# An mLSTM cell and a gated feed-forward in one kernel: another order of the first slot's rounding, sigmoid and transfers

## The chip, the cores and the metric

The kernel runs on one core of a Trainium2 chip. The metric is the device time of one execution in microseconds (us). The profiled core's TensorE clock was granted at 0.981 of full speed on average.

## The reference, cut to what matters

An mLSTM recurrence over 768 steps for 4 batches and 8 heads of 40 dimensions, then a feed-forward whose activation is h·cos(h):

```python
for t in range(S):
    m_new = np.maximum(f_gate[:, :, t] + m, i_gate[:, :, t])
    f_stab = np.exp(f_gate[:, :, t] + m - m_new)
    i_stab = np.exp(i_gate[:, :, t] - m_new)
    C = f_stab * C + i_stab * outer(vt, kt)
    n = f_stab * n + i_stab * kt
    y[:, :, t] = sigmoid(o_gate) * (C @ qt) / maximum(abs(n . qt), 1)
x = y.transpose(0, 2, 1, 3).reshape(B * S, H * D)      # 3072 x 320
h = x @ w_in                                           # 320 x 2048
out = (h * cos(h)) @ w_out                             # 2048 x 320
```

## The kernel before, in words

**Cells.** The sequence is cut into 6 chunks c of 128 steps. A chunk of one batch b is a cell n = 4c + b; there are 24. A cell computes scores (q times k, TensorE), weighs them with decays E (weigh, VectorE), multiplies by the values (values, TensorE), updates a state (seam, state) and normalises (normalize or normalize_turned). The result goes to xT, the input of the feed-forward for chunk c.

**Feed-forward.** Chunk c's feed-forward runs in 8 steps f2, each 2 times 128 of the 2048 columns. A step is an `Up`: matmuls of w_in with xT into two PSUM banks (L636, L639); then for each bank a rounding on ScalarE (near, L644), a subtraction on VectorE (rest, L647), a sine on ScalarE (sin, L652) and a product on VectorE (gate, L656). Both banks are free again after the gates, and only then may the next Up write them. The down step before it (down, L668) multiplies the gates by w_out.

**Slots.** After the head (first_cells: cells 0 to 3, in a hand-written order), both_parts(c, b) runs two Ups (i = 0 and i = 1) beside cell n = 4(c + 1) + b. The first slot is both_parts(0, 0), with cell 4 and the first two Ups of chunk 0; it also prepares cell 5. Each engine takes its instructions in the order in which the code names them; nothing is reordered. So an instruction that waits holds all that stands behind it on its engine.

**Weights.** w_in and w_out arrive as 64-bit floats and are made into float32 here. weights_in(f) loads the bits of 512 columns in three pieces (8 transfers of 128 KB and 4 of 64 KB, L139 and L174), weights_out(p) those of two row blocks in one (640 KB, L180). take_apart runs on ScalarE (L150, L152), put_together on VectorE (L157 to L161) and, last, on GpSimd (L162); to_float32 is both. `pieces` and `outs` hold what is loaded and not yet converted; next_out converts the next piece of w_out and loads another.

**Transfers.** All loads are issued by SyncE, in order, into one hardware queue; each is given one of eight completion slots in turn and waits for the transfer that had the slot before. load_E(n) brings the running maxima for a cell's decays (512 KB, L354), and for an even cell also the factors G for two cells (two times 256 KB, L360). load_two(n) brings q and k of two cells ("qk", L339) or k and v of two cells ("Kv", L344). The buffers ks2 and vs2 hold two cells each. load_o(1) brings the o gates of chunk 1 in 8 transfers (L309), and sigmoid(1) (L318, L320) turns them for all four cells of that chunk; turn_gate (L460) transposes them for one cell.

**For the next cell.** decay_exponents (L391, GpSimd) masks E, decay (L405, ScalarE) takes eight exponentials, weigh_k (L410) scales k, odd_values (L416, GpSimd) copies the upper dimensions of the values for an even cell and the odd one behind it, turn_blocks (L455, VectorE) transposes q and k of one cell, scale_q (L464, GpSimd) makes qG from the transposed q and G; values(n) reads qG and the copied values. clear_low (L440) zeroes two buffers once. sin_next (L938) makes ScalarE load the sine's table ahead of time. ScalarE loads a table whenever exponential, sigmoid and sine follow each other.

```python
def odd_values(n):
    if n % 2 == 0:
        src = vs2[n // 2 % 2].rearrange("q n (a g) d -> q (n a) g d", g=2)[:, :, :, 32:D]
        nc.gpsimd.tensor_copy(out=vr2[n // 2 % 2].rearrange("q n a g d o -> q (n a) g d o")[:, :, 0:3:2, :, 0], in_=src)
```

warm(k) issues k matmuls with zeros, which write a bank that nobody reads.

Of the kernel before, what the change touches and what calls it, by code (L numbers as in the profile page):

```python
# [29 lines left out]
def kernel(  # L30
# [23 lines left out]
    C = 128  # L54
# [87 lines left out]
    def to_float32(dst, bits):  # L142
        take_apart(dst, bits)
        put_together(dst, bits)
# [178 lines left out]
    def load(n, which="qkv"):  # L323
        c, b = divmod(n, B)
        for name, dst, src in (("q", qs(n), q), ("k", ks(n), k), ("v", vs(n), v)):
            if name in which:
                nc.sync.dma_start(out=dst[:, :, 0:D], in_=src[b, :, ts(c, C)].rearrange("h t d -> t h d"))

    def load_two(n, which="qkKv"):
        c, b = divmod(n, B)  # L330
        m = n // 2 % 2
        for name, src in (("q", q), ("k", k)):
            if name in which:
                src = src.rearrange("b (p j) (c t a) d -> j c t (b p) (a d)", j=2, a=C // 32, t=32)
                for j in range(2):
                    for low in range(1 if n < 2 * B else 2):
                        x = 0 if low else 32
                        dst = raws[name][m][64 * j + 32 * low:64 * j + 32 * low + 32, x:x + WR]
                        nc.sync.dma_start(out=dst.rearrange("t (p x) -> t p x", x=C // 32 * D),  # L339
                                          in_=src[j, c, :, 4 * b:4 * b + 8])  # L340
        for name, dst, src in (("K", ks2[m], k), ("v", vs2[m], v)):
            if name in which:
                src = src.rearrange("b h (c t) d -> c t b h d", t=C)
                nc.sync.dma_start(out=dst[:, :, :, 0:D], in_=src[c, :, b:b + 2])  # L344
# [472 lines left out]
    def first_cells():  # L817
        nc.vector.memset(nil, 0.0)
        gates_in()
        nc.scalar.copy(out=ident_b, in_=ident)  # L820
        load(0, "qk")
        later_gates_in()
        load(0, "v")
        load(1, "qk")
        load_o(0, (0, 1))
        load(1, "v")
        load(2, "qk")
        load_E(0)
        load_E(1)
        warm(12)  # L830
        wall_in(0, 0, pmu)
        wall_in(0, 1, psum_o())
        gates_first()
        gates_first_out()
        spread(0, 0)
        decay_exponents_half(0, 0)
        turn(0)
        turn_out(0, False)
        gates_sums()
        spread(0, 1)  # L840
        decay_exponents_half(0, 1)
        decay(0)
        weigh_k(0)
        load_E(2)
        load(2, "v")
        load_E(3)
        load_o(0, (2, 3))
        load(3)
        pieces.extend(weights_in(0))
        wall_in(1, 0, psum_o())  # L850
        wall_in(1, 1, psum_o())
        gates_less_sums()
        spread(1, 0)
        decay_exponents_half(1, 0)
        scores(0)
        gates_maxima()
        turn(1)
        weigh(0)
        sigmoid(0, slice(0, 2))
        turn_out(1, False)  # L860
        spread(1, 1)
        decay_exponents_half(1, 1)
        gates_exponents()
        decay(1)
        weigh_k(1)
        values(0)
        normalize(0)
        scores(1)
        gates_exp()
        turn(2)  # L870
        turn_out(2, False)
        warm(2)
        seam(0)
        weigh(1)
        seam_out(0)
        state(0)
        load_two(B, "qk")
        decay_exponents(2)
        gates_diagonal()
        decay(2)  # L880
        weigh_k(2)
        values(1)
        load_E(B)
        normalize(1)
        scores(2)
        turn(3)
        sigmoid(0, slice(2, 4))
        seam(1)
        load_two(B, "Kv")
        load_E(B + 1)  # L890
        load_o(1)
        outs.append((0, weights_out(0)))
        weigh(2)
        decay_exponents(3)
        turn_out(3)
        seam_out(1)
        values(2)
        decay(3)
        weigh_k(3)
        state(1)  # L900
        normalize(2)
        scores(3)
        pg = gates_turn()
        warm(1)
        seam(2)
        weigh(3)
        to_float32(*pieces.pop(0))
        decay_exponents(B)
        pieces.extend(weights_in(1))
        outs.extend((p, weights_out(p)) for p in range(1, 3))  # L910
        seam_out(2)
        state(2)
        for piece in pieces[0:2]:
            take_apart(*piece)
        gates_keep(*pg)
        values(3)
        normalize(3)
        put_together(*pieces.pop(0))
        warm(3)
        seam(3)  # L920
        seam_out(3)
        put_together(*pieces.pop(0))
        low_dimensions(B)
        turn_blocks(B)
        state(3)
        load_E(B + 2)
        decay(B)
        sigmoid(1)
        weigh_k(B)
        odd_values(B)  # L930
        scale_q(B)
# [14 lines left out]
    def both_parts(c, b):  # L946

        n = (c + 1) * B + b
        cell = n < N
        for i in range(2):  # L950
            f2 = 2 * b + i
            up = Up(c, f2)
            if cell and i == 0:
                scores(n)
                if c == 0 and b == 0:

                    warm(8, psum_o())
            if cell and i == 1:
                if n % 2 == 1 and n > B + 1 and n + 3 < N:
                    load_two(n + 3, "Kv")  # L960
            for e in range(2):
                up.near(e)
            for e in range(2):
                up.rest(e)
            if i == 0:
                if cell:
                    weigh(n)
                    if n + 1 < N:
                        decay_exponents(n + 1)
                    if n == B:  # L970
                        clear_low()
                for e in range(2):
                    up.sin(e)
                    up.gate(e)
                if c > 0:
                    sums(c, f2)
                if b == 0 and 0 < c < NC - 1:
                    sigmoid(c + 1)

                if c == 0 and b > 0 and pieces:  # L980
                    to_float32(*pieces.pop(0))
                if c == 0:
                    next_out()
                if cell and n + 1 < N:
                    decay(n + 1)
            else:
                if cell:
                    seam_out(n)
                if pieces:
                    to_float32(*pieces.pop(0))  # L990
                if cell:
                    state(n)
                for e in range(2):
                    up.sin(e)
                    up.gate(e)
                if c > 0:
                    sums(c, f2)
                if n == B + 1:
                    low_dimensions(n + 1)
                while pieces:  # L1000
                    to_float32(*pieces.pop(0))
                if cell and n + 1 < N:
                    weigh_k(n + 1)
                    odd_values(n + 1)
            down_slot(c, f2)
            if (c, f2) == (1, 0):
                weight_sums(1)
            if cell and i == 0:
                turn_gate(n)
                values(n)  # L1010
                seam(n)
                normalize_turned(n)
                fade(n)
                if n % 2 == 1 and n > B + 1 and n + 3 < N:
                    load_two(n + 3, "qk")
                if n > B + 1 and n + 3 < N:
                    load_E(n + 3)
                if b == B - 2 and c + 2 < NC:
                    load_o(c + 2)
                if c == 0 and pieces:  # L1020
                    to_float32(*pieces.pop(0))
                sin_next()
            if f2 == 0 and c > 1:
                for p in range(2):
                    combine(c - 1, p)
            if i == 1:
                if c == 0 and b + 2 < B:
                    pieces.extend(weights_in(b + 2))
                    load_two((n + 3) // 2 * 2)
                    load_E(n + 3)  # L1030
                if cell and n + 1 < N:
                    turn_blocks(n + 1)
                    scale_q(n + 1)
                if c == 0:
                    next_out()
                if (c, f2) == (0, LAST):
                    weight_sums(0)
# [41 lines left out]
```

## Time and profile before

| | |
|---|---|
| time, median of 3 runs | 556.17 us (553.79 to 556.29) |
| profiled execution: span from the first to the last instruction | 549.6 us |
| what lies around the span (runs less the span) | 4.1 to 6.6 us |
| PE / DVE / ACT / POOL busy | 522.2 / 420.0 / 280.4 / 235.3 us |
| first slot, first Up | 41.6 to 47.7 us |
| first slot, second Up | 58.2 to 63.0 us |
| DMA over the span | 57.81 MB, 105 GB/s |

The profiled execution has no time of its own beside its span; the three runs were timed without a profile. PE is TensorE, DVE VectorE, ACT ScalarE, POOL GpSimd, SP SyncE. A line of the timeline gives start, length, engine, source line, operation, the tiles written and read, the shape, how many, and in brackets how long the engine had been idle before and what ended that. A row of the windows gives the stretch, its length, each engine's busy time with the number of instructions, the granted clock of PE (1.00 is full), the mean busy share of the 16 DMA engines and GB/s. A share over 1 means that packets overlapped on an engine.

### The profile page before, as it was taken

The numbers are of one execution on the slowest core, as the hardware profiler recorded it, in microseconds if no ns is written. First come the engines' busy times: TensorE is split into PE (matmuls) and PEld (weight loads), VectorE is DVE, ScalarE is ACT, GpSimd is POOL, SyncE is SP. The second block draws the span as 40 slices with busy tenths as digits, with TensorE's granted clock in tenths as the row PEclk, the third lists the DMA queues.
The fourth block names the chain that finished last, engine by engine and source line by source line (L and its number), as shares of the span: only waits on it lengthen the run. The fifth ranks groups of instructions, "written<-read, shape, count | busy, mean of one in ns | idle before, by whom it ended". The sixth has DMA issues, their size and how long they took to land.

```text
span 549.6 us, 10494 instructions
## 1 busy us (share of the span) xinstructions
PE 522.2 (95%) x3844; PEld 348.6 (63%) x3844; DVE 420.0 (76%) x906; ACT 280.4 (51%) x537; POOL 235.3 (43%) x381
## 2 busy tenths in 40 slices
PE   7997989989979999999999999999999999999996
PEld 4873554546646666756766756766756757575755
DVE  5864999997877787887886888787887878674645
ACT  2867966847455445555535555535556533231311
POOL 7535456463784545534444435444423421221211
PEclk9968899999999999999999999999999999999999
DMA  9998878687926538318438428338410000010001
GB/s 135 228 201 224 244 163 215 137 188 186 163 92 155 72 92 187 41 67 202 49 93 183 44 67 199 52 92 181 47 69 25 5 6 6 1 48 1 1 1 48
DMA packets 99939, 57.81 MB, mean 105 GB/s; under 512 B 62304, under 2 KB 92608, under 8 KB 99888
## 3 DMA queue, kind: packets, MB, share of 16 engines
q1 hardware_dynamic: 96496, 55.64, 47.2%
q10 hardware_dynamic: 3248, 1.33, 1.1%
q8 instruction: 30, 0.49, 0.4%
q14 instruction: 21, 0.17, 0.1%
q0 software_dynamic: 144, 0.18, 0.1%
HBM read 51.71 MB, written 4.11 MB: 102 GB/s over the span
## 4 chain that ended last, share of the span: by engine, by line
PE 65%; DVE 11%; ACT 9%; POOL 5%; DMA 3%; issue 3%; SPq 3%; ACTq 0%; DVEq 0%; POOLq 0%
PE pup L636 24%; PE acc L746 21%; PE pup L639 7%; PE late L746 2%; PE ps L482 2%; DVE n L647 2%; ACT E L405 2%; DVE g L656 2%; PE vt L517 2%; PE po L668 2%; PE vt L508 1%; ACT n L644 1%; DMA E<-M_d 1%; DVE st L619 1%; DVE t L455 1%
## 5 line engine op out<-in xcount | busy, mean ns | idle before, releaser
L636 PE MATMUL pup<-xT,w_in_sb 128*128 128x512 f32 x384 | 178.8, 609 | 8.2 <-DVE g L656 7.8
L644 ACT ACTIVATE n<-pup 128x512 int32<-128x512 f32 x96 | 52.2, 595 | 206.4 <-PE pup L639 206.3
L647 DVE SCALAR_TENSOR_TENSOR n<-pup,n 128x512 f32<-128x512 f32 x96 | 61.8, 686 | 91.2 <-ACT n L644 91.2
L636 PEld LDWEIGHTS pup<-xT,w_in_sb 128*128 128x128 f32 x384 | 70.6, 192 | 84.2 <-issue 61.2
L710 POOL TENSOR_TENSOR D<-g 128x128 f32<-128x128 f32 x40 | 19.8, 495 | 178.6 <-DVE g L656 156.7
L652 ACT ACTIVATE n<-n 128x512 f32<-128x512 f32 x96 | 58.5, 631 | 18.5 <-DVE n L647 14.7
L656 DVE SCALAR_TENSOR_TENSOR g<-pup,n 128x512 f32<-128x512 f32 x96 | 61.7, 685 | 2.1 <-ACT n L652 0.4
L746 PE MATMUL acc<-w_out_sb,g 128*128 128x160 f32 x320 | 59.0, 305 | 0.0
L746 PE MATMUL acc<-T,g 128*128 128x160 f32 x320 | 58.3, 302 | 0.0
L639 PE MATMUL pup<-xT,w_in_l 64*128 64x512 f32 x192 | 54.2, 641 | 0.0
L746 PEld LDWEIGHTS acc<-w_out_sb,g 128*128 128x128 f32 x320 | 47.4, 190 | 6.8 <-issue 4.5
L746 PEld LDWEIGHTS acc<-T,g 128*128 128x128 f32 x320 | 47.8, 190 | 4.4 <-issue 3.8
L405 ACT ACTIVATE E<-E,tab 128x128 f32<-128x128 f32 x160 | 49.2, 391 | 2.0 <-POOL E L391 1.7
L668 PE MATMUL po<-w_out_sb,g 128*128 128x320 f32 x128 | 36.6, 439 | 3.8 <-POOL w_out_sb L162 3.7
L639 PEld LDWEIGHTS pup<-xT,w_in_l 64*128 64x128 f32 x192 | 14.4, 184 | 36.5 <-issue 34.3
L746 PE MATMUL acc<-T,S 128*128 128x160 f32 x160 | 35.3, 302 | 0.0
L538 POOL TENSOR_TENSOR yt<-yt,db 128x128 f32<-128x128 f32 x20 | 10.9, 545 | 55.0 <-DVE db L533 55.0
L668 PEld LDWEIGHTS po<-w_out_sb,g 128*128 128x128 f32 x128 | 23.7, 190 | 16.4 <-POOL w_out_sb L162 4.5
L482 PEld LDWEIGHTS ps<-t,t 40*128 40x128 f32 x384 | 24.8, 188 | 10.9 <-issue 8.0
L488 DVE TENSOR_TENSOR E<-ps,E 128x512 f32<-128x512 f32 x48 | 30.7, 681 | 0.0
L464 POOL TENSOR_TENSOR qG<-t,G 128x512 f32<-128x512 f32 x20 | 25.7, 1285 | 10.2 <-DVE t L455 10.0
L746 PE MATMUL acc<-w_out_sb,S 128*128 128x160 f32 x160 | 29.1, 301 | 0.0
(176 smaller groups left out, 902.5 us busy)
## 6 DMA issues: line engine op xcount, KB each, us to landing
E<-M_d SPq DMA_DIRECT2D x22, 512.0 KB
qr<-in_q_dram SPq DMA_DIRECT2D x36, 160.0 KB
kr<-in_k_dram SPq DMA_DIRECT2D x36, 160.0 KB
G<-G_d SPq DMA_DIRECT2D x20, 256.0 KB
bits<-in_moe_w_out_dram SPq DMA_DIRECT2D x8, 640.0 KB
bits<-in_moe_w_in_dram SPq DMA_DIRECT2D x32, 128.0 KB
out_dram<-o_sb SPq DMA_DIRECT2D x24, 160.0 KB
ks<-in_k_dram SPq DMA_DIRECT2D x10, 320.0 KB
```

Of the source, the lines that this page charges most:

```text
L405: nc.scalar.activation(out=Es[n][:, h], in_=Es[n][:, h], func=AF.Exp, scale=-1.0, bias=tab[:, c, 0, g:g + 1])
L464: nc.gpsimd.tensor_tensor(out=qG, in0=qkT[n][0], in1=Gs[n], op=OP.mult)
L482: nc.tensor.matmul(ps[j][:, p], kT[r, p], qT[r, p], start=True, stop=True)
L488: nc.vector.tensor_tensor(out=w, in0=pss[n][j], in1=w, op=OP.mult)
L636: nc.tensor.matmul(pu, w_in_sb[:, i, ts(2 * f2 + e, 128)], x(i), start=(i == 0), stop=False)
L639: nc.tensor.matmul(pu, w_in_l[r, f2], x(NK, r), start=False, stop=True)
L644: nc.scalar.activation(out=self.n[e], in_=self.pu[e], func=AF.Copy, bias=0.25)
L647: nc.vector.scalar_tensor_tensor(out=self.n[e].bitcast(FP), in0=self.pu[e], scalar=0.25, in1=self.n[e], op0=OP.add, op1=OP.subtract)
L652: nc.scalar.activation(out=r, in_=r, func=AF.Sin, scale=TWO_PI_DOWN)
L656: nc.vector.scalar_tensor_tensor(out=g, in0=self.pu[e], scalar=TWO_PI, in1=self.n[e].bitcast(FP), op0=OP.mult, op1=OP.mult)
L668: nc.tensor.matmul(po[c][b], gs[c, f][:, ts(b, C)], w_out_sb[:, f], start=(f == 0), stop=(f == NF - 1))
L746: nc.tensor.matmul(a, lhs, rhs, start=start, stop=stop)
```

## The change

In the head: k and v of cells 4 and 5 come in two pairs of transfers (load_one) and no longer in one pair; w_out's first piece is loaded ahead of the o gates; w_in's second group is loaded ahead of E for cell 5, and cell 5's k and v come behind E and w_out's second piece. values(3) and a put_together stand ahead of seam(2). One warm(3) becomes warm(1), so two warm matmuls fall away. sigmoid(1) leaves the head.

In the first slot: sigmoid(1) stands behind the first Up's sines and the conversion of w_out's first piece, where decay(5) stood; decay(5) and one more sin_next stand behind the second Up's gates; turn_blocks(5) moves from the end of the slot to behind the first Up's gates. All other slots keep their order. Lines of the changed kernel are 5 higher from load_two on.

```diff
+    def load_one(n):
+        c, b = divmod(n, B)
+        for dst, src in ((ks(n), k), (vs(n), v)):
+            nc.sync.dma_start(out=dst[:, :, 0:D], in_=src[b, :, ts(c, C)].rearrange("h t d -> t h d"))
...
         seam(1)
-        load_two(B, "Kv")
-        load_E(B + 1)
+        load_one(B)
+        outs.append((0, weights_out(0)))
         load_o(1)
-        outs.append((0, weights_out(0)))
...
         warm(1)
-        seam(2)
         weigh(3)
         to_float32(*pieces.pop(0))
         decay_exponents(B)
         pieces.extend(weights_in(1))
-        outs.extend((p, weights_out(p)) for p in range(1, 3))
-        seam_out(2)
-        state(2)
+        load_E(B + 1)
+        outs.append((1, weights_out(1)))
+        load_one(B + 1)
+        outs.append((2, weights_out(2)))
         for piece in pieces[0:2]:
             take_apart(*piece)
         gates_keep(*pg)
         values(3)
+        put_together(*pieces.pop(0))
+        seam(2)
+        seam_out(2)
+        state(2)
         normalize(3)
-        put_together(*pieces.pop(0))
-        warm(3)
+        warm(1)
         seam(3)
...
         decay(B)
-        sigmoid(1)
         weigh_k(B)
         odd_values(B)
         scale_q(B)
...
                 for e in range(2):
                     up.sin(e)
                     up.gate(e)
+                if (c, b) == (0, 0):
+                    turn_blocks(n + 1)
...
-                if cell and n + 1 < N:
+                if (c, b) == (0, 0):
+                    sigmoid(1)
+                elif cell and n + 1 < N:
                     decay(n + 1)
...
                 while pieces:
                     to_float32(*pieces.pop(0))
+                if (c, b) == (0, 0):
+                    decay(n + 1)
+                    sin_next()
...
                 if cell and n + 1 < N:
-                    turn_blocks(n + 1)
+                    if (c, b) != (0, 0):
+                        turn_blocks(n + 1)
                     scale_q(n + 1)
```

## The prediction

> **What bounds it now.** I read the windows first, then the timeline of the stretch that the diff touches (36 to 84 us), then the landing records of the transfers. The windows' columns are length, busy us of each engine, PE's granted clock, DMA share, GB/s.
>
> ```profile
> 37.00:52.00 15.00, 13.06 (x67) 6.60 (x66) 6.86 (x14) 9.00 (x25) 8.89 (x9) 0.76 1.07 218
> 52.00:60.00 8.00, 5.52 (x76) 4.20 (x77) 7.40 (x14) 7.94 (x15) 1.58 (x1) 0.79 0.67 228
> 60.00:100.00 40.00, 35.78 (x201) 19.82 (x200) 37.44 (x77) 28.18 (x54) 23.66 (x26) 1.00 0.84 199
> 100.00:150.00 50.00, 48.13 (x367) 28.52 (x367) 43.19 (x82) 32.19 (x57) 26.24 (x28) 1.00 0.83 169
> ```
>
> Up to 52 us the DMA queue is full. From 60 us DVE works 37.4 of 40 us, and after 100 us PE 48.1 of 50: what is late at 80 us is late at the end, for nothing later idles long enough to take it up. The first slot stalls here (start, length, engine, line, [idle before it]):
>
> ```profile
> 46.55 1.13 PE L639 MATMUL pup<-xT,w_in_l 64*128 64x512 f32 x4
> ...
> 49.08 1.28 ACT L318 ACT_TABLE_LOAD   x1 [2.60 <-issue]
> 50.37 1.06 ACT L318 ACTIVATE og<-o 128x1024 f32<-128x1024 f32 x1
> ...
> 51.87 1.09 ACT L644 ACTIVATE n<-pup 128x512 int32<-128x512 f32 x2
> ...
> 52.50 1.29 DVE L647 SCALAR_TENSOR_TENSOR n<-pup,n 128x512 f32<-128x512 f32 x2 [7.27 <-ACT n L644]
> ...
> 54.48 0.66 PE L508 MATMUL vt<-E,vs 128*32 128x128 f32 x8 [4.08 <-issue]
> ```
>
> The first Up is ready at 47.7, but its rounding (L644) stands behind the sigmoid, which waits for the o transfers until 48.8. DVE then waits 7.3 us and PE 4.1 before cell 4's values (L508).
>
> **What the change removes.** The rounding moves ahead of the sigmoid. It could start at 47.4 (first Up: PE frees 0.3 us earlier, since two warm matmuls of the head fall away), rest and weigh follow, and values(4) could start at 49.8, right behind the eight warm matmuls, not at 54.5. That alone is 4.7 us on PE.
>
> **What it adds: a wait on POOL.** POOL works in order, and in this stretch it has:
>
> ```profile
> 45.06 0.30 POOL L416 COPY vr<-vs 128x128 f32<-128x128 f32 x1
> 45.31 1.27 POOL L464 TENSOR_TENSOR qG<-t,G 128x512 f32<-128x512 f32 x1
> 46.53 1.09 POOL L391 TENSOR_SCALAR_AFFINE_SELECT E<-E 128x1024 f32<-128x1024 f32 x1
> ```
>
> odd_values(4) (L416) copies the odd values of cells 4 and 5 together, from the buffer vs. Before, one transfer brings both and lands at 42.74. Now cell 5's values are a transfer of their own, issued behind w_in's second group, E of cell 5 and w_out's second piece; it stands ahead of odd_values in the program, and in the changed program's waits the copy waits for it. Behind the copy on POOL stand qG(4), which values(4) need on PE; the select for cell 5, two memsets and w_out's first piece; and DVE's transposes for cell 5, now in the first half of the slot, overwrite what qG(4) reads, so they wait as well, with all of DVE's work behind them.
>
> **When do cell 5's values land (T)?** The trace's last landings of each transfer in the full queue: G 39.48, k and v of cells 4 and 5 42.74, E of cell 5 45.28, o 48.79, w_out 51.55, w_in 56.94, next w_out 59.21. The gaps are the prices: E 2.54, o 3.51, w_out 2.76 and 2.27, w_in 5.39. A single cell's k or v (L327 in the head) lands 0.83 to 1.2 us behind the one ahead of it, so a pair costs about 1.9. In the new order: 39.48 + 1.9 + 2.76 + 3.51 + 5.39 + 2.54 + 2.27 + 1.9 = 59.75. That is the upper end. Before, the queue was not full in part of this:
>
> ```profile
> 52.00:54.00 2.00, 0.00 (x0) 0.00 (x0) 1.50 (x3) 1.98 (x3) 0.00 (x0) 1.00 0.69 178
> 54.00:56.00 2.00, 1.52 (x32) 1.55 (x35) 2.00 (x4) 1.99 (x4) 0.00 (x0) 0.63 0.24 79
> 56.00:58.00 2.00, 2.00 (x42) 1.62 (x36) 1.93 (x5) 1.98 (x3) 0.00 (x0) 0.52 0.71 251
> ```
>
> The missing shares (0.31, 0.76 and 0.29 of 2 us) are 2.7 us; if the new order, with E behind the small pieces, fills all of it, T is 57.0. I take 58.5, a little over the middle: the sum is of measured gaps, the refill is only argued.
>
> **From T to the end.** POOL: copy 0.30, qG 1.28, gaps: qG(4) is done at T + 1.65 = 60.15.
>
> DVE from there, all in a row: transposes for cell 5, 2.05 (69.90 to 71.93 before); w_out's first piece 1.9; oT 0.9; normalize_turned 3.0; w_in's piece 1.9. So the second Up's rest (L647) starts at 69.9; before at 63.75.
>
> PE: 28 of values(4)'s 32 pairs are left, 2.84 at half clock (54.48 to 57.70 was the whole at 3.2) and 0.6 for seam(4): the second Up starts at 63.6. PE was idle from 50.2 to 60.15, which halves the clock. Before, a 4.1 us idle stretch was followed by 3.4 us at half (granted clock 0.63 and 0.52 in the windows above, 1.00 around them), and the full clock came back after 3.4 us of unbroken work. On that 3.4 us raster full clock is back at 64.8, and the second Up (4.75 at full) ends at 68.95; if the part-filled stretch to 61.4 were enough, 1.3 us sooner. Rounding it takes 0.75 until DVE can go on: 69.7. So DVE and PE arrive together, at 69.9, whichever way the clock goes: **6.15 late**. The Trainium skill (TensorE: Matmul & The Clock Gate, Part 1) says that the gate opens after a busy window of some 3.4 us and closes after an idle one, the windows running free. By that rule the part-filled window does not count and the sum is as it stands; by the other reading it would be 0.5 lower, as ACT would run ahead of DVE. The one gap before agrees with the rule (half for 3.41 us); a part-filled window no run here shows.
>
> Up to the second gate nothing else changes order, so gate is at 73.8 (67.70 + 6.1) and the third Up runs 74.4 to 79.2. DVE then lacks the transposes (2.05 saved). But ACT now has cell 5's decay here: it ends the sines at 72.85, w_in_l 0.75, exp's table 1.28, eight exponentials 2.46, the sine's table again 1.28 + 0.1, and only then w_out's second piece, 78.75 to 80.2. (Before, that piece was taken apart at 67.3, and the decay at 56.8 to 60.6.) One table load more in all, 1.28, lies in this row. DVE finishes the piece at 81.4, POOL at 83.0, before 76.30: down's second step is 6.7 late. Third rest 81.4 (74.51), third gate 83.95 (76.91): 6.9 to 7.0 late. From the fourth Up on all orders are as before.
>
> Other edits: values(3) ahead of seam(2) and the earlier w_in pieces on ACT and DVE move the first Up by 0.6 us or less, and E of cell 5 lands near 56; both lie under the wait up to 60.15 and cost nothing; without that cover the first would save 0.3. The o transfers come about 1 us earlier, w_out about 7; both lie under it too. SP issues two transfers more (0.45 each), behind a full queue. ACT's two xT transfers now wait for a landing each of cell 5's values and of E of cell 6 (T + 2.0 + 3.3 = 63.8), which is over before ACT gets there at 70. POOL's four pieces behind the wait (select 1.1, memsets 2.4, w_out 1.6, yt 0.5, fade 2.1) end at 70.4, ahead of w_in's pieces that it needs at 69.9 to 71.7: up to 0.5 of slack used, no more.
>
> **Sum:** T - 51.65 = **+6.85** at T = 58.5: a span of 549.6 + 6.85 = 556.45, and with what lies around it (549.6 against the median's 556.17, 6.6) **563.0**. At T = 57.0 and with the clock early +4.8, at 59.75 +8.1. The no-gain point is T = 51.65.
>
> **Rivals.**
> 1. *The queue drains at its best rate.* The best two microseconds moved 403 GB/s (58 to 60). The 4352 KB from G to cell 5's values (4.46 MB) would then take 11.1 us: T = 50.5, 1.1 faster, 555.0: not slower. It decides from 51.65 down. Against it: 37 to 52 us moved 218 GB/s at a share of 1.07, for most packets are under 512 B (62304 of 99939). The Trainium skill (DMA: Bandwidth & Descriptors, Specifications) gives about 358 GB/s as a core's share of HBM; an estimate from that is T = 51.9 and no change. The trace's full windows lie well under it. Chance 0.09, times from 555 to 559.
> 2. *The wait does not bind* (the copy goes with cell 4's values alone). Then DVE runs through from 47.9, and the second rest comes at 61.65; but the decay on ACT still holds w_out's second piece until 71.4, POOL ends it at 74.2, and down's second step gains 2.1: 554.2. So even the change as meant gives 2 us of the 4.7. Against it: the program's waits. Chance 0.06, half of it under 553.4.
> 3. *Worse:* SP itself is held, as at 33.91, where issuing one v transfer took 4.64 us (another at 78.52 took 2.01); ahead of cell 5's values this would put T 2 to 4.6 later, 565 to 567.6. Chance 0.08. For it: many small rows. Against it: each transfer is half as large now.
>
> **Numbers.** Forecast 0.77, rivals 0.09, 0.06, 0.08. 0.5% is 2.8 us, about what a measurement of this kernel tells from no change. Slower 0.85 (forecast and 3), within it 0.12 (1 and half of 2), faster 0.03. The range, 557.5 to 565.5, takes in both ends of T and of the clock, part of 1 and the near part of 3.
>
> **What would show it.** Right: L416's copy (now L421) with some 12 us of idle POOL before it, released by vs at 57 to 60; PE idle near 10 us inside values(4); the cell 5 transposes on DVE right behind qG(4), at 60; rounding of the first Up at 47 to 48; w_out's second piece on ACT behind a table load, near 79. Wrong: the copy at 45, or cell 5's values landing before 54; or a slot from 84 to 100 us in which the lateness shrinks, which would mean slack that I did not see.

## The result, and the profile after

The changed kernel takes **560.57 us** (median of four runs, 559.63 to 563.25) against 556.07 for the kernel before (four runs beside it, 553.79 to 556.29). The medians differ by 4.5 us. The ratio, taken from all these runs, is 1.0112 with a 95% interval of 1.0076 to 1.0148, which is 6.2 us (4.2 to 8.2): slower, by about 1%. The forecast was 563.0. The profiled execution took 560.36 us with a span of 558.6, which leaves 1.8 us around the span; the spans of the two profiles differ by 9.0 us, twice what the medians differ by. The run before_again below tells why.

The windows of the changed kernel, with the columns as before (length, PE, PEld, DVE, ACT, POOL busy, granted clock, DMA share, GB/s):

```profile
37.00:52.00 15.00, 11.14 (x88) 5.88 (x87) 9.47 (x18) 12.48 (x30) 4.25 (x4) 0.92 0.97 198
52.00:60.00 8.00, 0.00 (x0) 0.00 (x0) 0.00 (x0) 4.17 (x8) 0.00 (x0) 0.56 0.95 211
60.00:100.00 40.00, 33.53 (x232) 19.53 (x233) 34.51 (x70) 24.62 (x48) 23.88 (x26) 0.92 0.77 186
100.00:150.00 50.00, 47.30 (x301) 26.80 (x300) 43.77 (x87) 31.33 (x59) 24.34 (x28) 1.00 0.71 164
```

From 52 to 60 us PE, DVE and POOL do nothing at all; before, PE and DVE worked 5.5 and 7.4 of those 8 us. The queue is full (share 0.95 to 0.97) and moves 198 to 211 GB/s. From 52 to 60 us it is fuller than before (0.95 against 0.67) and yet moves less (211 against 228 GB/s). The timeline of the first slot says what they wait for:

```profile
45.96 1.08 ACT L649 ACTIVATE n<-pup 128x512 int32<-128x512 f32 x2
...
60.37 0.30 POOL L421 COPY vr<-vs 128x128 f32<-128x128 f32 x1 [17.54 <-DMA vs<-in_v_dram]
60.62 1.26 POOL L469 TENSOR_TENSOR qG<-t,G 128x512 f32<-128x512 f32 x1
...
61.92 1.14 DVE L460 STREAM_TRANSPOSE t<-qr 128x512 f32<-128x512 f32 x1 [11.60 <-POOL qG L469]
...
61.94 0.66 PE L522 MATMUL vt<-qG,st 128*32 128x128 f32 x8 [12.93 <-POOL qG L469]
...
81.20 1.14 DVE L157 TENSOR_SCALAR w_out_sb<-w_out_sb 128x640 f32<-128x640 f32 x1 [2.32 <-ACT w_out_sb L150]
...
83.86 1.56 POOL L162 TENSOR_TENSOR w_out_sb<-w_out_sb,bits 128x640 int32<-128x640 int32 x1 [1.87 <-ACT n L649]
```

The rounding (L649) comes 5.9 us sooner than before, right behind the first Up, as the change means it to. Some 1.3 of these 5.9 us are not the change's: the first Up's eight large matmuls took 3.67 us in place of 4.98, for the granted clock was at full from 39.4 us on in this execution and from 44.3 in the one before. Then POOL's copy (L421) waits 17.5 us for the v transfer, and DVE and PE wait 11.6 and 12.9 us for the qG behind it. In the page's table of groups the same idle time stands alone in two lines; its last columns are the idle time before a group and what ended most of it:

```profile
L522 PE MATMUL vt<-qG,st 128*32 128x128 f32 x480 | 24.8, 280 | 12.9 <-POOL qG L469 12.9
L460 DVE STREAM_TRANSPOSE t<-qr 128x512 f32<-128x512 f32 x20 | 22.0, 1101 | 12.5 <-POOL qG L469 11.6
```

480 matmuls of that form in the whole kernel have 12.9 us of idle time before them, and one wait made all of it.

| us from the span's start | before | predicted | after |
|---|---|---|---|
| sigmoid's table in the head (L314) | 25.41 | | 26.24 |
| first Up's rounding | 51.87 | 47.4 | 45.96 |
| cell 5's values have landed (T) | 42.74 | 58.5 | 60.23 |
| qG(4) is done | 46.58 | 60.15 | 61.88 |
| second Up's rest | 63.75 | 69.9 | 72.33 |
| w_out's second piece ends on POOL | 76.29 | 83.0 | 85.42 |
| third rest | 74.51 | 81.4 | 83.64 |
| third gate | 76.91 | 83.95 | 86.03 |
| span | 549.6 | 556.45 | 558.6 |

T is read from the landing records of the trace. From the third gate to the end both profiles take the same (472.7 and 472.6): nothing is made up later. In other executions that stretch takes up to 3.7 us more; before_again shows where.

### The profile page after: what moved, and what is told of

Read it like the earlier page. It is cut to its first block, busy times and chain, and to the rows that moved or that the text cites. A ratio compares the mean times of both kernels' runs of the same rounds, so it can differ in the third digit from the quotient of the medians.

```text
span 558.6 us, 10488 instructions
## 1 busy us (share of the span) xinstructions
PE 520.5 (93%) x3842; PEld 347.3 (62%) x3842; DVE 422.5 (76%) x906; ACT 281.2 (50%) x539; POOL 235.2 (42%) x381
## 2 busy tenths in 40 slices
DMA packets 99971, 57.81 MB, mean 104 GB/s; under 512 B 62336, under 2 KB 92640, under 8 KB 99920
## 4 chain that ended last, share of the span: by engine, by line
PE 60%; DVE 12%; ACT 8%; DMA 6%; POOL 6%; SPq 4%; issue 3%; ACTq 0%; DVEq 0%; POOLq 0%
PE pup L641 23%; PE acc L751 20%; PE pup L644 7%; PE late L751 2%; DMA bits<-in_moe_w_out_dram 2%; DVE n L652 2%; PE ps L487 2%; DMA vs<-in_v_dram 2%; ACT E L410 2%; PE vt L522 2%; DVE g L661 1%; PE vt L513 1%; SPq L139 1%; DVE t L460 1%; DVE st L624 1%
## 5 line engine op out<-in xcount | busy, mean ns | idle before, releaser
L649 ACT ACTIVATE n<-pup 128x512 int32<-128x512 f32 x96 | 52.1, 594 | 219.2 <-PE pup L644 219.1
L657 ACT ACTIVATE n<-n 128x512 f32<-128x512 f32 x96 | 58.5, 629 | 18.3 <-DVE n L652 14.5
L751 PEld LDWEIGHTS acc<-w_out_sb,g 128*128 128x128 f32 x320 | 47.4, 190 | 6.8 <-issue 4.5
L522 PE MATMUL vt<-qG,st 128*32 128x128 f32 x480 | 24.8, 280 | 12.9 <-POOL qG L469 12.9
L460 DVE STREAM_TRANSPOSE t<-qr 128x512 f32<-128x512 f32 x20 | 22.0, 1101 | 12.5 <-POOL qG L469 11.6
```

Of the source, the lines that this page charges most:

```text
L522: nc.tensor.matmul(vt[32 * a:32 * a + 32, i], state[:, ts(HP * i + a, 32)], Gs[n][:, a], start=False, stop=True)
L649: nc.scalar.activation(out=self.n[e], in_=self.pu[e], func=AF.Copy, bias=0.25)
L657: nc.scalar.activation(out=r, in_=r, func=AF.Sin, scale=TWO_PI_DOWN)
L751: nc.tensor.matmul(a, lhs, rhs, start=start, stop=stop)
```

## The experiments

The theory: the copy's wait for cell 5's values is the whole loss. The main rivals: the changed order of the computing makes it (cell 5's decay with one more table load ahead of w_out's second piece, the transposes in the first half), or the clock that falls to half while PE waits. Times of the kernel before differ a little from one measurement to the next, so each run is set against the kernel before in its own.

**before_again** is the kernel before, unchanged.

> The kernel before, unchanged, to learn what its span and its first slot are in another execution. The changed kernel's four runs have spans 1.75 us under their times. If that holds for this kernel too, its profiled execution of 549.6 was a quick one, and its runs at 554 to 556 have spans of 552 to 554.5. The other reading, that a span lies 4 to 6.6 us under the time for this kernel, expects 549.6 again beside a time near 556.

554.02 us; ratio 0.9997 (0.9975 to 1.0018). All its runs, and the 30 of the kernel before beside it, have a span 1.7 to 1.9 us under the time; spans go from 549.1 to 554.6. So the first profile, 549.6, was one of the quickest executions, some 551.4 us long. This run's profile has a span of 554.6, and 4.9 us of the 5.0 are there when the first Up ends. Its windows in the head:

```profile
15.00:20.00 5.00, 5.00 (x23) 4.30 (x21) 2.96 (x4) 3.77 (x6) 3.58 (x6) 0.50 1.05 256
20.00:25.00 5.00, 5.00 (x31) 4.70 (x31) 1.72 (x7) 2.14 (x3) 1.91 (x3) 0.50 0.91 169
25.00:30.00 5.00, 5.00 (x44) 4.00 (x42) 2.36 (x4) 2.66 (x8) 2.13 (x2) 0.67 0.90 214
```

The clock (third figure from the end) is at half for most of this stretch; in the first profile it was 1.00 up to 30 us, and at half from there to 44. The sigmoid's table is loaded at 30.69 (25.41), and the first Up ends at 52.61 (47.68). The o transfers land at the same time in both (48.69 and 48.79), so a late head shortens the wait that the change is aimed at. In before_again:

```profile
55.20 1.29 DVE L647 SCALAR_TENSOR_TENSOR n<-pup,n 128x512 f32<-128x512 f32 x2 [4.70 <-ACT n L644]
```

The rest comes 2.6 us behind the first Up, against 4.8 in the first profile; the second rest is 66.45, only 2.7 later than there. So the kernel makes up nearly half of the late head. At the third gate 2.75 us are left, at the fourth 4.3, and from 172 us on it is 5.0. The fourth gate is later because the down step (L668) behind the third Up ran partly at half clock in this profile (granted clock 0.50 from 79.55 to 82.96 us, first line) and not in the first profile (second line):

```profile
79.10 6.26 PE L668 MATMUL po<-w_out_sb,g 128*128 128x320 f32 x16 [2.19 <-POOL w_out_sb L162]
```

```profile
76.34 4.57 PE L668 MATMUL po<-w_out_sb,g 128*128 128x320 f32 x16 [2.18 <-POOL w_out_sb L162]
```

The wait ahead of it was the same. The changed kernel's profile has 4.57 us there too; the profiles of turn_back, copy_split, v_late and warm_fill have 5.98, 6.26, 6.26 and 7.34. The time from the third gate to the end lies between 472.6 and 476.3 us in the kept profiles; this step makes 1.4 to 2.8 us of the difference where it is slow.

**copy_split** takes the wait away and leaves all else.

```diff
-        if n % 2 == 0:
+        if n in (B, B + 1):
+            src = vs(n).rearrange("q (a g) d -> q a g d", g=2)[:, :, :, 32:D]
+            nc.gpsimd.tensor_copy(out=vr2[n // 2 % 2][:, n % 2, :, 0:3:2, :, 0], in_=src)
+        elif n % 2 == 0:
```

> The changed kernel, but odd_values copies each cell's half by itself: cell 4's where the copy stands now, cell 5's one part later, where the same line is called for cell 5. The result stays the reference's. All transfers and orders stay as changed. Theory 1 (the copy's wait for cell 5's values is the whole loss): cell 4's copy starts near 45 us in place of 60.4, PE does not idle over 2 us inside values(4), the second rest comes at 61.5 to 63 in place of 72.3, the third gate at 75 to 77 in place of 86.0, and the time is 553 to 555.5. Theory 2 (the loss lies in the order: decay(5) behind one more table load, ahead of w_out's second piece, and E of cell 5 late): the third gate stays over 82 and the time over 557.

554.74 us; ratio 1.0014 (0.9987 to 1.0042). The loss is gone with the wait. Cell 4's copy is back at its place, cell 5's comes in the second half of the slot:

```profile
42.62 0.24 POOL L421 COPY vr<-vs 128x64 f32<-128x64 f32 x1
...
72.05 0.25 POOL L421 COPY vr<-vs 128x64 f32<-128x64 f32 x1
```

The second rest is at 62.99, as expected, and the third gate at 77.58, 0.6 us outside what was expected. The span is 552.7, 3.1 over the first profile: 0.7 of it is there at the third gate, and 2.4 more at the fourth, 1.7 of them from the down step at half clock.

**compute_only** and **transfers_only** are the two halves of the change. The first is the changed kernel with these lines as they were, the second the kernel before with these lines alone:

```diff
-        load_two(B, "Kv")
-        load_E(B + 1)
-        load_o(1)
-        outs.append((0, weights_out(0)))
+        load_one(B)
+        outs.append((0, weights_out(0)))
+        load_o(1)
...
         pieces.extend(weights_in(1))
-        outs.extend((p, weights_out(p)) for p in range(1, 3))
+        load_E(B + 1)
+        outs.append((1, weights_out(1)))
+        load_one(B + 1)
+        outs.append((2, weights_out(2)))
```

> The changed kernel with the old transfers: k and v of cells 4 and 5 in one pair, E of cell 5 and w_out where they were. What is left of the change is the order of the computing. Theory 1 (the wait for cell 5's values, which comes from the transfers' order alone): values land near 43, the copy does not wait, the time is 553 to 555.5. Theory 2 (the order of decay(5), sigmoid and transposes costs): 557 to 560.

> The kernel before with the changed order of transfers alone; the computing keeps its old order, so the first Up's rounding still stands behind the sigmoid and cell 5's transposes at the end of the slot. Theory 1: the copy waits for cell 5's values until 58 to 60.5 here too, the third gate comes at 84 to 86.5, the time is 558.5 to 562. Theory 2 (the computing's order makes the loss): the copy's wait lies beside other work, the time is 555 to 557.

compute_only: 553.75 us, ratio 0.9996 (0.9975 to 1.0017). transfers_only: 558.62 us, ratio 1.0076 (1.0045 to 1.0107), with the copy at 60.10 behind 15.0 us of idle POOL and the third gate at 83.63, 0.4 sooner than expected. The order of the computing costs nothing by itself, and brings nothing; the order of the transfers makes the loss.

**v5_w_out** and **v5_w_in** move the landing alone: compute_only with cell 5's v as a transfer of its own, behind w_out's first piece or behind w_in's second group. E of cell 5 and the k transfers stay early.

```diff
-        load_two(B, "Kv")
+        load_two(B, "K")
+        load_v(B)
         load_E(B + 1)
         load_o(1)
         outs.append((0, weights_out(0)))
+        load_v(B + 1)
```

This is v5_w_out; in v5_w_in the last line stands behind `pieces.extend(weights_in(1))`. load_v(n) is load_one(n) without k.

> The changed order of computing with the old transfers (as in the run compute_only, 553.75), but cell 5's v is a transfer of its own behind w_out's first piece; k of both cells and E of cell 5 stay early. Only the landing T of cell 5's values moves. Theory 1 (the wait costs what T lies behind the point where cell 4's values would start, and nothing before that): T is 50.5 to 52, the copy waits until then where the head was quick and not where it was slow, the time is 553.5 to 556. Theory 2 (it is the late E of cell 5 and the pieces behind it that cost, not the copy's wait): as compute_only, 553 to 554.5. The two overlap here; the run v5_w_in parts them.

> As v5_w_out, but cell 5's v behind w_in's second group. Theory 1: T is 56.5 to 58.5, the copy on POOL waits until then whichever way the head ran, the qG matmuls of cell 4's values start some 1.7 us behind T, the time is 556 to 559. Theory 2 (the late E of cell 5, not the copy's wait): E is early here, so 553 to 554.5.

| | T | time | ratio (interval) |
|---|---|---|---|
| compute_only | 42.70 | 553.75 | 0.9996 (0.9975 to 1.0017) |
| v5_w_out | 50.89 | 553.82 | 1.0003 (0.9981 to 1.0025) |
| v5_w_in | 57.81 | 558.99 | 1.0104 (1.0074 to 1.0135) |

Each ratio is against the kernel before in the same measurement. Up to 50.9 us the landing costs nothing, at 57.8 it costs 1.04%, 5.8 us. In v5_w_in PE waits as it does in the changed kernel, with E of cell 5 there since 45.42, so that no late E can be the cause:

```profile
57.86 0.30 POOL L425 COPY vr<-vs 128x128 f32<-128x128 f32 x1 [13.77 <-DMA vs<-in_v_dram]
...
59.43 0.66 PE L526 MATMUL vt<-qG,st 128*32 128x128 f32 x8 [10.22 <-POOL qG L473]
```

The second rest is at 69.83, which is T + 12.0; the changed kernel has T + 12.1.

**v_mid** and **v_late** move cell 5's k and v within the changed kernel.

```diff
+        load_one(B + 1)
         load_E(B + 1)
         outs.append((1, weights_out(1)))
-        load_one(B + 1)
         outs.append((2, weights_out(2)))
```

This is v_mid; in v_late the line stands behind the last one shown.

> The changed kernel with k and v of cell 5 issued ahead of E of cell 5 and of w_out's second piece (right behind w_in's second group), so the 3.5 and 1.9 us that those two took in the queue no longer lie ahead of them. Theory 1 (everything from the copy on moves with the landing T, one for one): T is 54.5 to 55.5 in place of 60.23, the copy starts at once behind it, the third gate comes some 5 us sooner than 86.0, near 81, and the time is 555 to 557. Theory 2 (the loss is not T's): the third gate stays over 84 and the time over 559.

> The changed kernel with k and v of cell 5 issued one transfer later, behind w_out's third piece. Theory 1: T is 61.8 to 62.8, the third gate 1.6 to 2.6 later than 86.0, the time 562 to 563.5. Theory 2 (the loss is not T's): 559.5 to 561.

v_mid: 558.33 us, ratio 1.0088 (1.0059 to 1.0117). T is 55.27 and the copy starts at 55.32, as expected, but the third gate comes at 84.27, not near 81: a miss. E of cell 5, now behind, lands at 58.06, and POOL's select and two memsets follow it. Beside them DVE's first operation on w_out, 0.48 us when alone, takes 2.99:

```profile
58.12 1.09 POOL L396 TENSOR_SCALAR_AFFINE_SELECT E<-E 128x1024 f32<-128x1024 f32 x1 [1.28 <-DMA E<-M_d]
...
58.84 2.99 DVE L157 TENSOR_SCALAR w_out_sb<-w_out_sb 128x640 f32<-128x640 f32 x1
...
59.16 1.19 POOL L445 MEMSET qr<- 128x1312 f32 x1
...
60.29 1.19 POOL L445 MEMSET kr<- 128x1312 f32 x1
```

It ends 0.35 us behind the second memset. The time, 558.33, missed the 555 to 557 as well. This execution also had a late head (first Up ended at 52.41) and its third Up ran at half clock (6.42 us for the eight large matmuls), so it is no clean measure of T's price. v_late: 563.01 us, ratio 1.0181 (1.0147 to 1.0216). The time is as expected, but not for the reason given: T did not move (59.97), since E came earlier in that execution, and the third gate is at 85.77, no later than in the changed kernel. The profile's longer span (561.0) comes from behind it, 1.7 us of it from the down step at half clock. The run says nothing on the price of T.

**warm_fill** keeps PE at work during the wait: 60 warm matmuls in place of 8 ahead of cell 4's values.

```diff
-                    warm(8, psum_o())
+                    warm(60, psum_o())
```

> The changed kernel with 60 warm matmuls in place of 8 ahead of cell 4's values, so that PE works through the wait and its clock does not fall to half; the wait itself stays. Theory 1 (the wait holds DVE and POOL, and DVE sets the second rest; PE's half clock from 53 to 66.7 us lies beside it): the second Up ends 1 to 2 us sooner, the second rest stays within 0.7 us of 72.3, the time within 1 us of the changed kernel's 560.6. Theory 2 (a good part of the loss is the half clock): the second rest comes at 69.5 to 71, the time is 557 to 559.

563.97 us, ratio 1.0181 (1.0139 to 1.0223): slower, which neither theory expected. The clock was 1.00 from 52 to 80 us in the profile, but the head was late there, the warm matmuls ran on past qG (done at 62.1), and cell 4's qG matmuls started at 66.37. The third gate is at 87.64, 1.6 us later than in the changed kernel, and the down step behind it took 7.34 us. Three of its six runs took 560.95 to 562.25, the changed kernel's own range, and three 565.7 to 566.2. That full clock during the wait brings no gain is what the quicker three suggest; the run does not show it. The changed kernel's own profile speaks for it: there the second rest (72.33) follows DVE's work on w_in's piece without idle time, while the rounding was done at 71.92, so the half clock was not what the rest waited for.

**turn_back** puts turn_blocks(5) back at the end of the slot, in the changed kernel.

```diff
-                if (c, b) == (0, 0):
-                    turn_blocks(n + 1)
...
-                    if (c, b) != (0, 0):
-                        turn_blocks(n + 1)
+                    turn_blocks(n + 1)
```

> The changed kernel with turn_blocks(5) back at the end of the slot; the copy still waits for cell 5's values. Theory 1 (with the wait in force all of DVE's work stands behind qG(4), so the 2.05 us of transposes moved into the first half make the second rest that much later): w_out's first piece on DVE no longer waits for qG(4), the second rest comes at 70 to 70.8 in place of 72.3, as in the run transfers_only (70.48), the third gate at 83.5 to 85, the time is 558 to 559.5. Theory 2 (the place of the transposes does not count): 560 to 561.5.

561.61 us, ratio 1.0134 (1.0101 to 1.0167): my theory of it fell. DVE was ready at 69.0, but the second Up was not:

```profile
64.77 4.83 PE L641 MATMUL pup<-xT,w_in_sb 128*128 128x512 f32 x8
...
71.33 1.29 DVE L652 SCALAR_TENSOR_TENSOR n<-pup,n 128x512 f32<-128x512 f32 x2 [2.35 <-ACT n L649]
```

Its eight matmuls took 4.83 us (3.70 at full clock), and DVE waited 2.35 us for the rounding. With the wait in force DVE and PE limit the second rest nearly together, and taking 2 us from one gains little.

**w_out_first** and **warm_up3** ask why compute_only gains nothing. The first is compute_only with w_out's second piece converted ahead of cell 5's decay; the second adds to that 14 warm matmuls ahead of the third Up. The two edits:

```diff
                 if (c, b) == (0, 0):
+                    to_float32(*outs.pop(0)[1])
                     decay(n + 1)
                     sin_next()
...
-                if c == 0:
+                if (c, b) == (0, 0):
+                    outs.append((4, weights_out(4)))
+                elif c == 0:
                     next_out()
```

```diff
             f2 = 2 * b + i
+            if (c, f2) == (0, 2):
+                warm(14, ps_a.tile([128, HP, C], FP, name="pm", tag="a"))
             up = Up(c, f2)
```

> The changed order of computing with the old transfers (as in the run compute_only), and in the first slot w_out's second piece converted ahead of cell 5's decay and its two table loads on ScalarE; its follow-up load stays at the end of the slot. Theory 1 (what eats the gain of the earlier rounding is that decay(5) holds w_out's second piece): the piece is taken apart at 66 to 68 in place of 72.1, DVE has no wait of 2.3 us for it, down's second step and the third gate come 1 to 2.5 us sooner against the end of the first Up, the time is 551.5 to 553. Theory 2 (the gain is lost elsewhere: DVE's longer block up to the second gates, and the third Up at half clock behind an idle PE): third Up still at half clock, the third gate moves by under 0.7, the time is 553 to 554.5.

> The run w_out_first (553.14) with 14 warm matmuls ahead of the third Up, where PE idled 4.2 us and the third Up then ran at half clock in part (5.08 us for eight matmuls in place of 3.7). Theory 1 (this half clock is the last thing that eats the gain of the earlier rounding): the third Up takes 3.7 us, DVE's wait of 3.15 us ahead of the third rest falls to 1.8, the time is 551 to 552.3, faster than both kernels. Theory 2 (the gain is taken up further on): 552.8 to 554.

The third Up and what DVE waits for at that place, in compute_only, w_out_first and warm_up3:

```profile
69.21 6.30 PE L641 MATMUL pup<-xT,w_in_sb 128*128 128x512 f32 x8 [4.17 <-DVE g L661]
...
72.92 1.17 DVE L157 TENSOR_SCALAR w_out_sb<-w_out_sb 128x640 f32<-128x640 f32 x1 [2.27 <-ACT w_out_sb L150]
```

```profile
67.20 5.08 PE L641 MATMUL pup<-xT,w_in_sb 128*128 128x512 f32 x8 [4.17 <-DVE g L661]
...
74.00 1.29 DVE L652 SCALAR_TENSOR_TENSOR n<-pup,n 128x512 f32<-128x512 f32 x2 [3.15 <-ACT n L649]
```

```profile
66.65 3.19 PE L820 MATMUL pm<-nil 128*128 128x512 bf16 x14
71.00 3.67 PE L641 MATMUL pup<-xT,w_in_sb 128*128 128x512 f32 x8 [1.16 <-DVE g L661]
...
76.39 1.29 DVE L652 SCALAR_TENSOR_TENSOR n<-pup,n 128x512 f32<-128x512 f32 x2 [1.74 <-ACT n L649]
```

w_out_first: 553.14 us, ratio 1.0001 (0.9974 to 1.0029). DVE's wait for ScalarE is gone, and a longer wait for the third Up stands in its place: from the first Up's end to the third gate it takes 27.8 us, compute_only 29.0, but the time shows nothing. warm_up3: 551.51 us, ratio 0.9973 (0.9946 to 1.0000). The third Up is back at 3.67 us and the same stretch takes 26.4. It is the only version that comes out ahead of both kernels, by 0.27% or 1.5 us, at the edge of what the measurement can tell. The profile is no clean support: with a head as late as in before_again (first Up ended at 52.43) its span is 551.4 against 554.6, but of these 3.2 us only 0.9 are there at the third gate; the others come behind it, where before_again has its down step at half clock. So why compute_only gains nothing stays open in part.

## Why the prediction came out as it did

**The mechanism was right.** A wait that the change adds on POOL takes the place of the one it removes on ScalarE, and copy_split takes the whole loss away by splitting one copy of 0.30 us. Each instruction named as held was held: the copy, qG(4), DVE's transposes, PE inside values(4).

**The landing T was 1.7 us too early** (58.5 against 60.23). The last landings of the changed kernel are: G 39.84, k and v of cell 4 41.00, w_out 43.49, o 46.72, w_in 53.56, E 57.06, next w_out 58.94, k and v of cell 5 60.23. From G to T that is 20.39 us; my sum of gaps was 20.27. The gaps themselves moved (w_in 6.84 in place of 5.39, E 3.50 for 2.54, the others less), but their sum held. What failed is the refill that I took off it: I read a missing busy share (2.7 us, of which I credited 1.25) as room for more bytes. The new order did raise the share from 52 to 60 us, from 0.67 to 0.95, and the rate fell from 228 to 211 GB/s; from G on the same 4352 KB took 20.39 us, 19.73 before. Why the fuller queue moved less stays open. T lies 0.5 us behind even the plain sum (59.75), mostly because G landed 0.36 us later.

**From T to the second rest** I had 11.4 us and the trace has 12.1. w_out's first piece took DVE 3.0 us (63.85 to 66.84, where the next operation starts), not 1.9, beside POOL's memsets, which the wait had put there. That PE and DVE would arrive together holds within 1 us, as turn_back shows.

**The clock** went, in this stretch, as the prediction read the cited rule of the Trainium skill (TensorE: Matmul & The Clock Gate, Part 1). The changed kernel, by windows of 3.41 us:

```profile
53.04:56.45 3.41, 0.00 (x0) 0.00 (x0) 0.00 (x0) 3.15 (x7) 0.00 (x0) 0.50 0.93 240
56.45:59.87 3.42, 0.00 (x0) 0.00 (x0) 0.00 (x0) 0.00 (x0) 0.00 (x0) 0.50 1.16 218
59.87:63.28 3.41, 1.34 (x28) 1.25 (x32) 1.36 (x2) 0.00 (x0) 2.91 (x4) 0.50 0.95 328
63.28:66.69 3.41, 3.41 (x46) 2.29 (x39) 3.34 (x4) 0.00 (x0) 1.91 (x2) 0.50 0.59 151
66.69:70.00 3.31, 3.31 (x9) 1.33 (x10) 3.23 (x12) 0.00 (x0) 1.57 (x1) 1.00 0.15 19
```

The part-filled window (PE busy 1.34 of 3.41 us) does not bring the clock back, the full one behind it does. Full clock came back at 66.69 and not at 64.8. The 64.8 had no ground: it carried the places of the windows over from the profile of before, and they lie elsewhere in each execution (full clock came back at 62.68 in v5_w_in and at 67.09 in turn_back). That the second Up still took 5.36 us, as summed (5.35), is luck: it began 1.85 us later than forecast, and the clock came back 1.9 later.

**From the second rest to the third gate** 14.05 us were expected and 13.7 came. The order on ScalarE was as forecast: w_out's second piece, behind cell 5's decay and its tables, was there at 80.40 (78.75, later by what T is later).

**What lies around the span was mis-sized.** I added 6.6 us, the median less the span of before; 1.8 is right, because the profiled execution was quicker than the median. The span's sum was 2.15 us too low (556.45 against 558.6) and this term 4.8 too high: the two together are the 2.6 by which 563.0 stands over the profiled execution's 560.36. That the forecast came within 2.5 us of the median, 560.57, is in part luck, then: two errors of opposite sign. With 1.8 in place of 6.6 the same sum gives 558.2.

**Why the medians differ by less than the spans.** T does not follow the head: in transfers_only, copy_split, the changed kernel, turn_back, v_late and warm_fill it is 59.55 to 60.43, while the first Up ends anywhere between 45.9 and 52.3. In a quick execution the wait therefore costs more: set off against a head 0.83 us later, the profiles give 9.0 - 0.8 = 8.2. Against before_again the second rest is T + 12.1 - 66.45 = 5.9 us late; the spans differ by 4.0 there, since before_again loses more behind the third gate. The measured ratio's 6.2 us (4.2 to 8.2) and the medians' 4.5 lie between 4.0 and 8.2.

**The rivals.** *Queue at its best rate:* fell, 198 to 211 GB/s. *The wait does not bind:* copy_split builds it, and 554.2 was close (554.74), but I counted that as a gain of 2 us on 556.17; against the kernel before in the same measurement it is none. Three terms were missed. From ScalarE's start on w_out's second piece to POOL's end on it copy_split takes 5.0 us (71.99 to 76.96), where I had 2.8 (71.4 to 74.2). PE can fall to half clock behind an idle stretch: the third Up took 6.30 us for 3.70 in compute_only, the down step 6.26 for 4.57 in copy_split. And the o gates make the kernel before wait for less in executions with a late head. *SP held:* it was held for 4.26 us at 34.62 and 4.51 at 54.05, issuing w_out pieces, but not at a place that moved T by the 2 to 4.6 us of this rival.

## What to carry to other kernels

When a transfer for two users is split so that the first half comes early, look for every instruction that still reads both halves: here one copy of 0.30 us held three engines. For a wait on a full queue, add up the measured gaps between landings and take nothing off for a better fill until a trace shows it: a higher busy share of the DMA engines moved no more bytes here. Set a sum against the profiled execution's own time, and take a second profile of the same kernel before reading a difference of 1% between two spans, and look where the clock fell to half in each.

## What the runs showed of the hardware

DVE's tensor_scalar (L157) took longer beside POOL: on w_out, where it takes 0.48 us alone, 1.68 us in the changed kernel and 2.99 in v_mid; on a piece of w_in, 0.42 us alone, 2.34 in copy_split. Each time it ended 0.28 to 0.35 us behind the second of POOL's memsets. The Trainium skill (SBUF — State Buffer, Who interferes with whom) says that a tensor_scalar can run in a 2-port mode, and that such an instruction and a GpSimd instruction exclude each other for the whole of one instruction. The times agree; in which mode it ran no run here shows. In v_mid DVE was not let in between a select and two memsets in a row. In copy_split it ended at 60.51, when POOL's next instruction (60.20 to 61.91) was already under way.

The head's clock fell to half with PE busy 5.00 of 5 us (before_again, 15 to 25 us), at another place in each execution: the first Up ends anywhere between 45.9 and 52.6 us. What sets that off no run here shows.

Behind the head a change of the clock always came a whole number of 3.41 us windows after the one before, but a window need not be idle to cost the clock. One with PE busy 0.99 to 1.26 us was followed by half clock in turn_back, v_late, before_again and copy_split; one with 1.70 us was not in the changed kernel. At half clock a window with 2.83 us brought the full clock back in w_out_first, one with 2.55 did not in copy_split. What differs is where the windows lie: behind the same 2.4 us of idle PE the down step took 4.57 us in the changed kernel and 6.26 in v_late.
